# DeltaNet into a GELU MLP on one core: where the row steps stand between the weight groups, and the order of the head

## The chip, the cores and the metric

The kernel runs on one core of one Trainium2 chip. The metric is the device time of that core in microseconds (us), from its first to its last instruction. The kernel before takes 669.52 us, the median of three runs (669.08 to 671.37). The core has five engines that work side by side, each through its own list of instructions in order: PE (TensorE, matmuls), DVE (VectorE), ACT (ScalarE), POOL (GpSimd) and SP (SyncE, which issues most DMAs here). They wait for each other by semaphores only.

## The reference

Attention state by the delta rule, for 4 batches, 8 heads, 768 steps, head size 48; then a two-layer MLP with an exact GELU over 3072 tokens (384 to 2048 to 384). All is f32, but the two weight matrices come as float64.

```python
k_n = k / (np.linalg.norm(k, axis=-1, keepdims=True) + 1e-06)
for t in range(S):
    y[:, :, t] = einsum('bhd,bhde->bhe', q[:, :, t], state)
    v_old = einsum('bhde,bhd->bhe', state, k_n[:, :, t])
    state = state + beta[:, :, t] * einsum('bhd,bhe->bhde', k_n[:, :, t], v[:, :, t] - v_old)
x = y.transpose(0, 2, 1, 3).reshape(B * S, H * D)
h = x @ w_in
out = (0.5 * h * (1.0 + erf(h / sqrt(2)))) @ w_out
```

## The kernel before

**Chunks.** The 768 steps are cut into 12 chunks of 64 (`C`). Two batches share the 128 partitions, so a chunk is two units (`NA`), `tiles[c, a]`. Inside a chunk the recurrence becomes matrices: the gram matrix of the keys (`grams`, psG), the queries against the keys (`queries`, P), and a unit triangular system for each head that is inverted. Chunks go by pairs, called groups (`g`). For a group, `eliminate_steps(g)` inverts the 32x32 diagonal blocks of all heads on DVE: `scales` and `flip` bring the blocks into one tile Nu, 30 pairs of `row_product` (L492) and `row_sum` (L497) do the substitution one row after the other, each needing what the one before wrote; `diagonal` and `back` (L506, L510) turn the result into XM and Zf. `join` makes of two 32-blocks one of 64 by two matmuls (psJ), with a product on DVE between (L542, later L583).

**A chunk's pass.** `against_state` multiplies the keys and queries with the state (psK) and W = (psK - V) times factors on DVE (L658, L659). `solve` gives U (psU), `use` gives the output psY and the state's change (`update`), `next_state` adds it on DVE (L708), `read` copies the output to x, and `turn` transposes x into xT (psX, L740). V has to be scaled by the norm of its key first: of chunk 0 in `ng`, of chunk 1 by POOL (`scale_v`, L362), of chunks 2 and 3 by ACT, one head at a time (`scale_head`, L357), of the later ones by POOL. `prep(c)` makes the squares of a chunk's keys on ACT (L303), their sums on DVE (L308) and the root on POOL (L334); `finish(c)` turns them into factors on DVE.

**The MLP.** `fc1` is one of 16 tiles of the first layer (psH, L763), its GELU on ACT writes G (L765). `fc2` is the second layer (psO, L776) for chunks 0 and 1; later chunks use a scheme with seven half products (L801), with sums of w_out on DVE (`sums_of_w`, L787).

**The weights.** The float64 words come in as pairs of 32-bit words and are decoded on chip, in 16 groups of 128 x 768: groups 0 to 7 are w_in, 8 to 15 w_out. `fetch(n)` loads a group's raw words, into four places in w_out_sb for w_in, into three slots for w_out; a place is loaded again when its group has been scaled. A group takes five DVE steps and one on ACT: `begin` (L220, exponent bits), `exponents` on ACT (L225), `upper` (L229), `lower` (L234), `sign` (L242, needs ACT's exponent) and `scaled` (L246). `decode_steps(first, last)` orders them so that the steps of group n and n + 1 alternate.

**What sets the order.** The head, up to the first decoded groups, is written out by hand for all engines (`by_hand`), so program order there is engine order. After it, a plan of steps with times is sorted: `on(a, b, steps)` spreads steps over a stretch on the author's own scale of time, `once(t, ...)` puts them at one time, `at` does the same on a scale of chunks. Up to `late`, DVE and ACT run in the plan's order; after it DVE alone. On the other engines a scheduler orders what the plan emits, except where `together` ties matmuls to each other and where `keep_in_program_order` holds an ACT instruction in its place. `late` frees the memory and banks of the first stage, and clears two tiles Kb on ACT (L1007) that lie there; the first layer of chunk 1 has 12 tiles ahead of it (`EARLY`) and 4 behind it.

Of the kernel before, what the change touches and what calls it, by code (L numbers as in the profile page):

```python
# [16 lines left out]
def kernel(  # L17
# [158 lines left out]
    mask_h = mask.unsqueeze(1).to_broadcast([128, H, C])  # L176
    Zf = [cpool.tile([128, NU, C], F32, name=f"Zf{i}") for i in range(2)]
    G = cpool.tile([128, NF, NA * 128], F32)
    for p in range(2):
        nc.gpsimd.memset(Zf[0][p * C + HB:(p + 1) * C, :, 0:HB], 0.0)  # L180
    St = cpool.tile([128, NA, 2, NP, D], F32)
    nc.vector.memset(St, 0.0)
    nc.scalar.activation(lim[:, 1:2], lim[:, 0:1], ACT.Gelu)
# [101 lines left out]
    def new_group(g):  # L285
        gms[g] = wk.tile([128, 2 * NA, H], F32, tag="gm", name="gm")
# [9 lines left out]
    def squares(u, n, engine=None):  # L296
        kd = u.Kn[:, :, 0:D]
        if engine is nc.gpsimd:
            ksq = su.tile([128, H, D], F32, tag="w_e", name="ksq")
        else:  # L300
            ksq = wk.tile([128, H, D], F32, tag="ksq", name="ksq")
        if engine is None:
            i = nc.scalar.activation(ksq, kd, ACT.Square)  # L303
            if u.c == 4:
                tc.keep_in_program_order(i)
        else:
            engine.tensor_tensor(ksq, kd, kd, op=ALU.mult)
        nc.vector.tensor_reduce(n, ksq, axis=AX.X, op=ALU.add)  # L308
# [52 lines left out]
    def scale_v(u, engine=nc.gpsimd):  # L361
        engine.tensor_tensor(u.V, u.V, ns[u.c][:, u.a].unsqueeze(2).to_broadcast([128, H, D]),  # L362
                                op=ALU.mult)

    def transposed(u, part=(0, 1)):
        for x in part:
            if x == 0:
                dst = u.Kt = wk.tile([128, 2, NP, C], F32, tag="Kt", name="Kt", bufs=6)
            elif u.c == 1:
                dst = u.Qt = su.tile([128, 2, NP, C], F32, tag="Qt1", name="Qt1")  # L370
            else:
                dst = u.Qt = wk.tile([128, 2, NP, C], F32, tag="Qt", name="Qt")
# [178 lines left out]

    def copy_out(name, n):
        for dst, src in copies[name][:n]:
            tc.keep_in_program_order(nc.scalar.copy(dst, src))
        del copies[name][:n]

    def join_run(g, ts0, ts1):
# [354 lines left out]
    for n in range(2):  # L912
        fetch(n)
    load_k(2, "Kp")
    new_group(0)
    n0 = wk.tile([128, 2 * NA, H], F32, tag="n0", name="n0", bufs=1)
    for c in range(2):
# [10 lines left out]
    scales_, flip_, *rows, back0, back1 = [s_[1:] for s_ in eliminate_steps(0)]  # L928
    factors(gms[0], beta_m[:, 0:2].rearrange("q c a h -> q (c a) h"), n0)
    scales_[0]()  # L930
    flip_[0]()
    ng = wk.tile([128, NA, H], F32, tag="n", name="ng", bufs=4)
    for u in first:
        grams([u])
    signs(2, NC)
    for u in first:
        transposed(u, (1,))
        queries([u])
        for h in range(4 * u.t, 4 * u.t + 4):
            sum_of_squares(tiles[2, h // H], h % H)  # L940
    for a in range(NA):
        fetch_in(tiles[2, a].Qp[:, :, 0:D], q, tiles[2, a])
    for a in range(NA):
# [2 lines left out]
        fetch(n)  # L946
    for n in range(n_in, n_in + len(slots)):
        fetch(n)
    load_v(1)
    third = [tiles[2, a] for a in range(NA)]  # L950
    for u in third:
        transposed(u, (0,))
    grams(third)
    for u in third:
        transposed(u, (1,))
    fourth = [tiles[3, a] for a in range(NA)]
    for u in fourth:
        transposed(u, (0,))
    grams(fourth)
# [10 lines left out]
    left(0, range(NA))  # L970
    for a in range(NA):
        join(0, (a,), 1)
    for step in copies.pop("diag"):
        nc.scalar.copy(*step)
    for u in first[NA:]:
        scale_v(u)
    for n in range(2):
        begin(n)
    for n in range(2):
        exponents(n)  # L980
    for n in range(2):
        mantissas(n)
    solve(first[:NA])
    signed(0)
    use(first[:NA])
    for u in first[:NA]:
        read(u)
    signed(1)
    for u in first[:NA]:
        turn(u)  # L990
    begin(2)
    exponents(2)
    mantissas(2)
    signed(2)
    by_hand.close()
    tc.no_sync_barrier()

# [21 lines left out]
    def fc1s(c, f, n, first, last):  # L1019
# [1 line left out]

    zero, one, b = first[:NA], first[NA:], range(NA, 2 * NA)
    rows1, join1 = eliminate_steps(1), join_steps(1)
    plan = [fc1s(0, 0, 4, 57.0, 63.0), fc1s(0, 4, 2, 65.0, 67.8), fc1s(0, 6, 2, 69.0, 71.8),
            fc1s(0, 8, 4, 73.6, 79.0), fc1s(0, 12, 2, 80.0, 82.8), fc1s(0, 14, 2, 85.4, 88.0)]
    plan += [once(63.2, (together, *[(update, u) for u in zero], (join, 0, b, 0)),
                  *[(next_state, u) for u in zero]),
             once(64.2, (left, 0, b)), once(68.3, (together, (join, 0, b, 1))),
             once(72.2, (together, (against_state, one))), once(75.2, (subtract, one)),
             once(79.2, (together, (solve, one))), once(83.2, (together, (use, one))),  # L1030
             once(84.6, *[(read, u) for u in one]), once(86.0, *[(next_state, u) for u in one]),
             once(88.1, *[(turn, u) for u in one])]
    plan += [on(57.8, 72.0, [(1.0, sum_of_squares, tiles[3, a], h)
                             for a in range(NA) for h in range(H)]),
             once(73.0, (load, 3), (prep, 2), (prep, 3))]
    decode = decode_steps(3, NW)
    ends = [3 + 5 * i for i in range(NW - 2)]
    plan += [on(56.8, 60.6, decode[:ends[1]]), on(60.6, 65.0, decode[ends[1]:ends[2]]),
             on(66.5, 70.8, decode[ends[2]:ends[3]]), on(70.8, 75.0, decode[ends[3]:ends[4]]),
             on(76.8, 81.0, decode[ends[4]:ends[5]]), once(81.1, (finish_both,), *[s_[1:] for s_ in rows1[:2]]),  # L1040
             on(84.2, 125.8, alternate(decode[ends[5]:], rows1[2:-3])), once(128.6, (late,))]
    for i in range(NF // 2):
        t = 89.7 + 5.2 * i
        plan += [on(t, t + 2.5, [(1.0, fc2, u, 2 * i, 2 * i + 2) for u in zero])]
        if i < EARLY // 2:
            plan += [fc1s(1, 2 * i, 2, t + 2.6, t + 5.1)]
    plan += [fc1s(1, EARLY, NF - EARLY, 128.7, 132.0),
             on(131.5, 164.0, ffn_steps(1)[4:])]
    plan += [at(c + 1, c + 2, ffn_steps(c)) for c in range(2, NC)]
    plan += [on(91.0, 124.0, [(1.0, scale_head, tiles[2, a], h) for a in range(NA) for h in range(H)]),  # L1050
             on(133.0, 150.0, [(1.0, scale_head, tiles[3, a], h) for a in range(NA) for h in range(H)])]
    s2 = state_steps(2)
    plan += [once(126.7, *[s_[1:] for s_ in rows1[-3:-1]]),
             once(131.6, (together, (against_state, third))), once(131.7, (subtract, third)),
             once(133.0, (together, join1[0])), once(133.1, rows1[-1][1:]),
             once(136.0, (together, join1[1]), (copy_out, "join", 4)),
# [30 lines left out]
    for w in range(3, NC):  # L1087
        two_ahead = w + 2 < NC
        if w % 2:
            if w == 3:  # L1090
                plan += [at(w + 0.09, w + 0.092, [(1.0, transposed, u, (1,)) for u in fourth]
                            + [(1.0, together, *gram(5))])]
            plan += [at(w + 0.25, w + 0.95, state_steps(w, (), query(w)))]
            if two_ahead:
                rows = eliminate_steps(w // 2 + 1)
                plan += [at(w - 0.16, w - 0.15, [(1.0, prep, w + 2)]),
                         at(w, w + 0.01, [(1.0, finish, w + 2)]),
                         at(w + 0.13, w + 0.18, rows[:2]), at(w + 0.18, w + 0.36, rows[2:26]),
                         at(w + 0.4, w + 1.06, rows[26:-3]), at(w + 1.07, w + 1.2, rows[-3:])]
# [48 lines left out]
```

## Time and profile before

| | before |
|---|---|
| time, median of 3 | 669.52 us |
| profiled execution, span | 666.2 us |
| PE busy | 633.7 us (95%) |
| DVE busy | 441.3 us (66%) |
| ACT busy | 223.7 us (34%) |
| POOL busy | 82.3 us (12%) |
| decode, sign (L242), mean of one | 0.95 us |
| row product (L492), mean of one | 0.34 us |

A line of the page's groups or of the timeline names the line of the kernel, the engine, the operation, out<-in by tile, shapes and count, and times; a bracket behind it says how long the engine had been idle and what ended that. L numbers are lines of the kernel before; in the kernel after, the lines from 180 to 554 stand two lower, and then within six.

### The profile page before, as it was taken

How to read it: one execution, taken by the hardware profiler on the slowest of the kernel's cores; microseconds unless marked ns; L12 is line 12 of the kernel's file. 1: busy time of each engine (PE TensorE's matmuls, PEld its weight loads, DVE VectorE, ACT ScalarE, POOL GpSimd, SP SyncE). 2: the span in 40 equal slices, each digit the busy share in tenths (PEclk: the TensorE clock that was granted, in tenths of full speed). 3: DMA queues.
4: the chain of work that ended last, by engine and by line, in shares of the span. 5: the costliest groups of instructions: out<-in, count | busy, mean ns of one | idle time of the engine just before them, and what ended most of it. 6: DMA issues, size and time to landing. Idle time of an engine off the chain costs nothing.

```text
span 666.2 us, 20430 instructions
## 1 busy us (share of the span) xinstructions
PE 633.7 (95%) x8902; PEld 555.5 (83%) x8902; DVE 441.3 (66%) x920; ACT 223.7 (34%) x600; POOL 82.3 (12%) x81
## 2 busy tenths in 40 slices
PE   6678998899999999999999999999999999999997
PEld 5566875666589989989989989989989989989997
DVE  6989999956759865578755678755678754324022
ACT  3476653334352126232136132136032133131220
POOL 5043210002401011211011211011301010000000
PEclk9986999989999999999999999999999999999999
DMA  9696554122533233521233521212301210100101
GB/s 133 156 273 173 110 104 142 47 43 46 99 46 61 49 44 51 83 43 26 53 46 49 82 42 25 51 23 37 60 12 20 55 18 3 25 2 2 25 0 25
DMA packets 158426, 39.68 MB, mean 60 GB/s; under 512 B 150016, under 2 KB 153216, under 8 KB 158336
## 3 DMA queue, kind: packets, MB, share of 16 engines
q1 hardware_dynamic: 152464, 33.40, 26.6%
q10 hardware_dynamic: 5872, 4.97, 3.4%
q8 instruction: 70, 1.15, 0.7%
q14 instruction: 20, 0.16, 0.1%
HBM read 33.62 MB, written 4.72 MB: 58 GB/s over the span
## 4 chain that ended last, share of the span: by engine, by line
PE 78%; DVE 9%; DMA 4%; SPq 3%; ACT 2%; issue 1%; POOL 1%; ACTq 0%; POOLq 0%
PE psH L763 33%; PE psX L801 12%; PE psY L801 12%; PE psZ L801 4%; PE psK L645 3%; PE psG L397 3%; PE psO L776 3%; PE psJ L571 2%; SPq L96 2%; PE psY L694 2%; PE psU L675 2%; DMA w_out_sb<-in_moe_w_in_dram 2%; DMA Kp<-in_k_dram 1%; SPq L212 1%; DVE Nu L497 1%
## 5 line engine op out<-in xcount | busy, mean ns | idle before, releaser
L763 PE MATMUL psH<-xT,w_in_sb 128*128 128x256 f32 x1152 | 260.9, 384 | 2.9 <-ACT G L765 2.3
L763 PEld LDWEIGHTS psH<-xT,w_in_sb 128*128 128x128 f32 x1152 | 217.4, 191 | 36.5 <-ACT G L765 4.1
L765 ACT ACTIVATE G<-psH 128x256 f32<-128x256 f32 x192 | 73.1, 382 | 177.3 <-PE psH L763 162.5
L497 DVE TENSOR_TENSOR Nu<-Nu,tmp 128x30 f32<-128x30 f32 (+9 forms) x180 | 62.0, 344 | 5.0
L492 DVE TENSOR_TENSOR tmp<-Nu 128x30 f32<-128x30 f32 (+9 forms) x180 | 60.6, 336 | 5.0
L801 PE MATMUL psX<-w_out_sb,G 128*128 128x192 f32 x320 | 55.8, 328 | 0.0
L801 PE MATMUL psY<-w_out_sb,G 128*128 128x192 f32 x304 | 54.1, 329 | 1.1
L740 ACT COPY xT<-psX 128x384 f32<-128x384 f32 x24 | 11.5, 479 | 126.1 <-PE psX L739 124.7
L801 PEld LDWEIGHTS psX<-w_out_sb,G 128*128 128x128 f32 x320 | 52.4, 190 | 0.6
L801 PEld LDWEIGHTS psY<-w_out_sb,G 128*128 128x128 f32 x304 | 49.1, 190 | 3.2 <-DVE u L847 3.2
L776 PE MATMUL psO<-w_out_sb,G 128*128 128x384 f32 x128 | 46.5, 511 | 5.0 <-DVE w_out_sb L246 4.3
L334 POOL TENSOR_TENSOR n<-n,half 128x16 f32<-128x16 f32 x10 | 30.9, 3086 | 127.2 <-DVE n L308 105.0
L810 DVE TENSOR_TENSOR S<-G 128x512 f32<-128x512 f32 x20 | 13.8, 691 | 46.5 <-ACT G L765 46.1
L776 PEld LDWEIGHTS psO<-w_out_sb,G 128*128 128x128 f32 x128 | 23.9, 196 | 21.9 <-DVE w_out_sb L246 6.7
L658 DVE TENSOR_TENSOR W<-psK,V 128x384 f32<-128x384 f32 x22 | 12.2, 553 | 41.8 <-ACT y L657 41.2
L460 POOL MEMSET Zf<- 32x512 f32 x20 | 10.4, 518 | 194.7 <-DVE Zf L510 128.7
L815 DVE TENSOR_TENSOR G<-G 128x512 f32<-128x512 f32 x20 | 13.7, 691 | 24.9 <-PE psX L801 24.9
L801 PE MATMUL psY<-T,G 128*128 128x192 f32 x160 | 28.2, 329 | 0.0
L801 PE MATMUL psZ<-T,S 128*128 128x192 f32 x160 | 28.1, 329 | 0.0
L801 PE MATMUL psX<-T,G 128*128 128x192 f32 x160 | 28.1, 329 | 0.0
L362 POOL TENSOR_TENSOR V<-V,n 128x384 f32<-128x384 f32 x18 | 16.1, 905 | 84.7 <-DMA V<-in_v_dram 64.0
L801 PEld LDWEIGHTS psZ<-T,S 128*128 128x128 f32 x160 | 26.1, 190 | 0.3
(146 smaller groups left out, 856.2 us busy)
## 6 DMA issues: line engine op xcount, KB each, us to landing
Kp<-in_k_dram SPq DMA_DIRECT2D x76, 96.0 KB, 3.2
w_out_sb<-in_moe_w_in_dram SPq DMA_DIRECT2D x24, 256.0 KB, 4.3
V<-in_v_dram SPq DMA_DIRECT2D x48, 96.0 KB, 3.3
out_dram<-o_sb ACTq DMA_DIRECT2D x46, 96.0 KB, 2.2
w_raw<-in_moe_w_out_dram SPq DMA_DIRECT2D x10, 384.0 KB, 3.9
Zf<-in_moe_w_out_dram SPq DMA_DIRECT2D x6, 384.0 KB, 4.5
Qp<-in_q_dram SPq DMA_DIRECT2D x64, 32.0 KB, 2.2
Qp<-in_q_dram SPq DMA_DIRECT2D x16, 96.0 KB, 4.3
```

The lines of the kernel that those rows point to most:

```text
L334: nc.gpsimd.tensor_tensor(flat, flat, half, op=ALU.pow)
L362: engine.tensor_tensor(u.V, u.V, ns[u.c][:, u.a].unsqueeze(2).to_broadcast([128, H, D]), op=ALU.mult)
L397: nc.tensor.matmul(psG[HALF[p], r, i * NP + j, :], lhsT=u.Kt[rows, p, j, :], rhs=(u.Qt if x else u.Kt)[rows, p, j, :], start=True, stop=True)
L492: nc.vector.tensor_tensor(tmp, nu[:, j + 1:, j:j + 1].to_broadcast([128, n, j]), nu[:, j:j + 1, 0:j].to_broadcast([128, n, j]), op=ALU.mult)
L497: nc.vector.tensor_tensor(nu[:, j + 1:, 0:j], nu[:, j + 1:, 0:j], tmps.pop(j), op=ALU.add)
L645: nc.tensor.matmul(u.psK[to, x, r, j, :], lhsT=(u.Qt if x else u.Kt)[rows, p, j, :], rhs=St[rows, u.a, p ^ r, j, :], start=True, stop=True)
L763: nc.tensor.matmul(psH, lhsT=w_in_sb[:, f // 2, m, f % 2 * 128:(f % 2 + 1) * 128], rhs=xTs[c][:, m, :], start=(m == 0), stop=(m == NM - 1))
L765: nc.scalar.activation(G[:, f, :], psH, ACT.Gelu)
L776: nc.tensor.matmul(u.psO, lhsT=G[:, f, u.a * 128:(u.a + 1) * 128], rhs=w_out_sb[:, f, :], start=(f == 0), stop=(f == NF - 1))
L801: nc.tensor.matmul(ps_, lhsT=lhs[:, f, :], rhs=rhs[:, f, :], start=first and f == 0, stop=f == FH - 1, skip_group_check=not first)
L810: nc.vector.tensor_tensor(W2["S"][:, fs], a21, a22, op=ALU.add)
L815: nc.vector.tensor_tensor(a12, a12, a11, op=ALU.subtract)
```

## The change

It touches the head and the first three chunks.

- Row steps of group 1: before, they alternate with the last seven and a half weight groups, up to the last decode step. After, the plan decodes up to group 9 without them, and puts the first 40 row steps between groups 10 to 15; the last 20 follow behind the last decode step. `finish_both` and the first two steps move behind group 9.
- Decoding of groups 0 to 2: the steps of groups 0 and 1 go in pairs (begin, begin, upper, upper, ...), and group 2 is part of the alternating order from its start, so that no step needs the one just ahead of it.
- The head's transposes of the queries run one tile ahead of the products that use them; of chunk 2, one transpose goes ahead of the grams.
- V of chunk 1 is loaded earlier, behind K of chunk 2, and scaled by ACT in the head, head by head; POOL's two instructions go.
- Times of the plan's other steps up to chunk 3 are set anew: six tiles of fc1 ahead of the first join, the first pair of fc2 ahead of chunk 1's turn, prep of chunk 5 later, with its squares kept in program order on ACT. The lower copies of diag for chunk 3 and the clearing of a part of Zf go later.

```diff
-    for p in range(2):
-        nc.gpsimd.memset(Zf[0][p * C + HB:(p + 1) * C, :, 0:HB], 0.0)
...
             i = nc.scalar.activation(ksq, kd, ACT.Square)
-            if u.c == 4:
+            if u.c < 6:
                 tc.keep_in_program_order(i)
...
     load_k(2, "Kp")
+    load_v(1)
...
     scales_[0]()
+    for p in range(2):
+        nc.gpsimd.memset(Zf[0][p * C + HB:(p + 1) * C, :, 0:HB], 0.0)
     flip_[0]()
...
-    for u in first:
-        transposed(u, (1,))
+    transposed(first[0], (1,))
+    for u, ahead in zip(first, first[1:] + [None]):
+        if ahead is not None:
+            transposed(ahead, (1,))
         queries([u])
         for h in range(4 * u.t, 4 * u.t + 4):
             sum_of_squares(tiles[2, h // H], h % H)
+        for h in range(4 * u.t, 4 * u.t + 4):
+            scale_head(tiles[1, h // H], h % H)
...
-    for step in copies.pop("diag"):
-        nc.scalar.copy(*step)
-    for u in first[NA:]:
-        scale_v(u)
-    for n in range(2):
-        begin(n)
-    for n in range(2):
-        exponents(n)
-    for n in range(2):
-        mantissas(n)
+    for step in (begin, exponents, upper, lower):
+        for n in range(2):
+            step(n)
     solve(first[:NA])
-    signed(0)
+    sign(0)
+    sign(1)
...
-    signed(1)
+    scaled(0)
+    scaled(1)
...
-    begin(2)
-    exponents(2)
-    mantissas(2)
-    signed(2)
+    decode = decode_steps(2, NW)
+    for _, fn, *args in decode[:3]:
+        fn(*args)
...
-    plan = [fc1s(0, 0, 4, 57.0, 63.0), fc1s(0, 4, 2, 65.0, 67.8), fc1s(0, 6, 2, 69.0, 71.8),
-            fc1s(0, 8, 4, 73.6, 79.0), fc1s(0, 12, 2, 80.0, 82.8), fc1s(0, 14, 2, 85.4, 88.0)]
+    plan = [fc1s(0, 0, 6, 57.0, 63.2), fc1s(0, 6, 2, 65.2, 67.8), fc1s(0, 8, 2, 69.2, 71.8),
+            fc1s(0, 10, 4, 74.9, 79.1), fc1s(0, 14, 2, 80.5, 83.1)]
...
-    plan += [on(56.8, 60.6, decode[:ends[1]]), on(60.6, 65.0, decode[ends[1]:ends[2]]),
-             on(66.5, 70.8, decode[ends[2]:ends[3]]), on(70.8, 75.0, decode[ends[3]:ends[4]]),
-             on(76.8, 81.0, decode[ends[4]:ends[5]]), once(81.1, (finish_both,), *[s_[1:] for s_ in rows1[:2]]),
-             on(84.2, 125.8, alternate(decode[ends[5]:], rows1[2:-3])), once(128.6, (late,))]
+    plan += [on(54.3, 57.9, group(2)), on(57.9, 61.4, group(3)), on(61.4, 65.0, group(4)),
+             on(67.5, 71.0, group(5)), on(71.0, 74.6, group(6)), on(76.8, 80.4, group(7)),
+             on(80.4, 84.0, group(8)), on(84.0, 87.5, group(9)),
+             once(87.8, (finish_both,), *[s_[1:] for s_ in rows1[:2]]),
+             on(91.9, 126.0, alternate(group(10, NW - 1), rows1[2:42])),
+             on(126.1, 128.4, rows1[42:-3]), once(128.6, (late,))]
     for i in range(NF // 2):
-        t = 89.7 + 5.2 * i
+        t = (84.2, 88.3)[i] if i < 2 else 92.1 + 5.68 * (i - 1)
...
-                plan += [at(w - 0.16, w - 0.15, [(1.0, prep, w + 2)]),
+                plan += [at(w - (0.05 if w == 3 else 0.16), w - (0.04 if w == 3 else 0.15), [(1.0, prep, w + 2)]),
```

More of the change, by code (lines that the diff above doesn't have):

```diff
@@ L553, in copy_out @@
         for dst, src in copies[name][:n]:
-            tc.keep_in_program_order(nc.scalar.copy(dst, src))
+            i = nc.scalar.copy(dst, src)
+            if name != "diag":
+                tc.keep_in_program_order(i)
         del copies[name][:n]
@@ L948 @@
         fetch(n)
-    load_v(1)
     third = [tiles[2, a] for a in range(NA)]
+    fourth = [tiles[3, a] for a in range(NA)]
     for u in third:
         transposed(u, (0,))
+    transposed(third[0], (1,))
     grams(third)
-    for u in third:
-        transposed(u, (1,))
-    fourth = [tiles[3, a] for a in range(NA)]
+    transposed(third[1], (1,))
     for u in fourth:
@@ L1023, with group @@
     rows1, join1 = eliminate_steps(1), join_steps(1)
-    plan = [fc1s(0, 0, 4, 57.0, 63.0), fc1s(0, 4, 2, 65.0, 67.8), fc1s(0, 6, 2, 69.0, 71.8),
-            fc1s(0, 8, 4, 73.6, 79.0), fc1s(0, 12, 2, 80.0, 82.8), fc1s(0, 14, 2, 85.4, 88.0)]
-    plan += [once(63.2, (together, *[(update, u) for u in zero], (join, 0, b, 0)),
+    def group(n, last=None):
+        return decode[3 + 5 * (n - 2):3 + 5 * ((last or n) - 1)]
+    plan = [fc1s(0, 0, 6, 57.0, 63.2), fc1s(0, 6, 2, 65.2, 67.8), fc1s(0, 8, 2, 69.2, 71.8),
+            fc1s(0, 10, 4, 74.9, 79.1), fc1s(0, 14, 2, 80.5, 83.1)]
+    plan += [once(65.05, (together, *[(update, u) for u in zero], (join, 0, b, 0)),
                   *[(next_state, u) for u in zero]),
-             once(64.2, (left, 0, b)), once(68.3, (together, (join, 0, b, 1))),
-             once(72.2, (together, (against_state, one))), once(75.2, (subtract, one)),
+             once(66.2, (left, 0, b), (copy_out, "diag", 2)), once(68.0, (together, (join, 0, b, 1))),
+             once(71.9, (together, (against_state, one))), once(74.7, (subtract, one)),
              once(79.2, (together, (solve, one))), once(83.2, (together, (use, one))),
-             once(84.6, *[(read, u) for u in one]), once(86.0, *[(next_state, u) for u in one]),
-             once(88.1, *[(turn, u) for u in one])]
+             once(85.2, *[(read, u) for u in one]), once(87.6, *[(next_state, u) for u in one]),
+             once(87.7, *[(turn, u) for u in one])]
     plan += [on(57.8, 72.0, [(1.0, sum_of_squares, tiles[3, a], h)
@@ L1035 @@
              once(73.0, (load, 3), (prep, 2), (prep, 3))]
-    decode = decode_steps(3, NW)
-    ends = [3 + 5 * i for i in range(NW - 2)]
-    plan += [on(56.8, 60.6, decode[:ends[1]]), on(60.6, 65.0, decode[ends[1]:ends[2]]),
-             on(66.5, 70.8, decode[ends[2]:ends[3]]), on(70.8, 75.0, decode[ends[3]:ends[4]]),
-             on(76.8, 81.0, decode[ends[4]:ends[5]]), once(81.1, (finish_both,), *[s_[1:] for s_ in rows1[:2]]),
-             on(84.2, 125.8, alternate(decode[ends[5]:], rows1[2:-3])), once(128.6, (late,))]
+    plan += [on(54.3, 57.9, group(2)), on(57.9, 61.4, group(3)), on(61.4, 65.0, group(4)),
[4 more added lines that the diff above has]
+             on(126.1, 128.4, rows1[42:-3]), once(128.6, (late,))]
     for i in range(NF // 2):
-        t = 89.7 + 5.2 * i
+        t = (84.2, 88.3)[i] if i < 2 else 92.1 + 5.68 * (i - 1)
         plan += [on(t, t + 2.5, [(1.0, fc2, u, 2 * i, 2 * i + 2) for u in zero])]
+        t = max(t + 2.6, 88.8)
         if i < EARLY // 2:
-            plan += [fc1s(1, 2 * i, 2, t + 2.6, t + 5.1)]
+            plan += [fc1s(1, 2 * i, 2, t, t + 2.5)]
     plan += [fc1s(1, EARLY, NF - EARLY, 128.7, 132.0),
-             on(131.5, 164.0, ffn_steps(1)[4:])]
+             on(131.5, 164.0, ffn_steps(1)[NF - EARLY:])]
     plan += [at(c + 1, c + 2, ffn_steps(c)) for c in range(2, NC)]
@@ L1052 @@
     s2 = state_steps(2)
-    plan += [once(126.7, *[s_[1:] for s_ in rows1[-3:-1]]),
+    plan += [once(128.5, *[s_[1:] for s_ in rows1[-3:-1]]),
              once(131.6, (together, (against_state, third))), once(131.7, (subtract, third)),
```

## The prediction

> **What bounds the kernel now.** I read the busy shares in 40 slices first, then the stretches of the opening 150 us, then VectorE's (DVE's) timeline in them, and last who waited for whom.
>
> ```profile
> PE   6678998899999999999999999999999999999997
> ...
> DVE  6989999956759865578755678755678754324022
> ...
> PEclk9986999989999999999999999999999999999999
> ```
>
> From slice 12 on (200 us) PE, TensorE, is 9 in every slice but the last, so the rest of the program has a fixed length: what counts is when it begins. Before, slices 2 to 8 are DVE's.
>
> ```profile
> 85.82:90.34 4.52, 4.52 (x140) 3.93 (x139) 4.16 (x9) 1.22 (x4) 1.91 (x1) 1.00 0.63 111
> 90.34:136.37 46.03, 40.34 (x157) 28.13 (x156) 44.08 (x100) 17.67 (x45) 0.00 (x0) 0.97 0.33 93
> 136.37:140.50 4.13, 4.13 (x14) 2.50 (x13) 4.04 (x5) 0.48 (x1) 0.00 (x0) 0.97 0.01 1
> 140.50:148.30 7.80, 6.67 (x142) 5.41 (x144) 0.03 (x1) 3.42 (x8) 0.00 (x0) 1.00 0.47 79
> ```
>
> (Columns: PE, PE's weight loads, DVE, ACT = ScalarE, POOL = GpSimd, each busy us and count; clock; DMA.) DVE is 96% busy until the last weight group is decoded, and empty right behind it. The timeline of DVE and PE there:
>
> ```profile
> 134.20 0.95 DVE L242 SCALAR_TENSOR_TENSOR w_e<-w_raw,w_e 128x768 uint32<-128x768 uint32 x1
> 135.07 0.21 DVE L497 TENSOR_TENSOR Nu<-Nu,tmp 128x58 f32<-128x58 f32 x1
> 135.32 0.19 DVE L492 TENSOR_TENSOR tmp<-Nu 128x30 f32<-128x30 f32 x1
> 135.42 0.95 DVE L246 SCALAR_TENSOR_TENSOR w_out_sb<-w_out_sb,w_e 128x768 f32<-128x768 f32 x1
> 136.57 2.07 DVE L506 STREAM_TRANSPOSE XM<-Nu 128x1024 f32<-128x1024 f32 x1
> 138.54 1.90 DVE L510 STREAM_TRANSPOSE Zf<-Nu 128x1024 f32<-128x1024 f32 x1
> 148.27 0.56 DVE L658 TENSOR_TENSOR W<-psK,V 128x384 f32<-128x384 f32 x1 [7.83 <-ACT y L657]
> ...
> 132.91 7.12 PE L776 MATMUL psO<-w_out_sb,G 128*128 128x384 f32 x16 [2.34 <-DVE w_out_sb L246]
> 143.74 2.86 PE L763 MATMUL psH<-xT,w_in_sb 128*128 128x256 f32 x12 [1.13 <-ACT G L765]
> ```
>
> The chain to read: last decode (ends 136.3), second layer of chunk 0 (psO, ends 140.0), its copies and sends, PE free at 143.74. The row steps (L492, L497) between the decode steps are needed by nobody until psJ at 148.54. DVE then idles 7.83 us: that is the room for them.
>
> **What the Trainium skill says.** "VectorE: DVE Perf Modes", section "The DRAIN you can't avoid": a next op waits until the pipe is empty, but "a next op that is not held starts earlier". The trace shows both:
>
> ```profile
> 28.11 0.41 DVE L497 TENSOR_TENSOR Nu<-Nu,tmp 128x238 f32<-128x238 f32 x1
> 28.55 0.41 DVE L492 TENSOR_TENSOR tmp<-Nu 128x240 f32<-128x240 f32 x1
> ...
> 71.49 0.95 DVE L234 SCALAR_TENSOR_TENSOR w_in_sb<-w_out_sb,w_in_sb 128x768 f32<-128x768 uint32 x1
> 72.36 0.55 DVE L220 TENSOR_SCALAR w_e<-w_out_sb 128x768 uint32<-128x768 uint32 x1
> ```
>
> Row steps need what stands just ahead: 0.41 long, the next after 0.44. The decode ops here do not: 0.95 long, the next after 0.87. So a dependent neighbour costs about 0.11 us. "GPSIMD Engine Reference", section "1. Specifications": its SBUF interfaces are shared with VectorE. The trace agrees: while POOL scales V (49.85 to 52.49) two decode ops take 1.47 and 1.58 instead of 0.95. "TensorE: Matmul & The Clock Gate", Part 1, gives half clock after an idle window; here the clock is 0.50 from 48 to 61 us and again at 134 to 136.
>
> **The change part by part.** A full decode step of one group costs 0.47+0.87+0.47+0.87+0.87 = 3.55 us from start to start (timeline, 72.36 to 75.90).
>
> 1. Groups 0 to 3. The steps of a group are begin (L220), upper (L229), lower (L234), sign (L242), scaled (L246). Before, DVE goes from the first begin at 47.33 to the end of lower of group 3 at 62.37. After: two ops of each kind at a time, 3.62 for begins, uppers, lowers and 3.48 for signs and scales, ending 54.4; no V on POOL, so no stretching. Then start 2, upper 2, lower 2, start 3: 2.4, at 56.8. Sign 2 needs ACT's exponent, which stands on ACT behind the copies of xT, and those behind psU (ended 51.98) by 6.56 us; psU had a hole of 1.55 us that no semaphore explains. With less DMA then (the fetches leave some 5 us earlier, as the Q tiles come free earlier) I take 0.5 off: exponent at 58.0, so a wait of 1.2. Ends: no wait, or 1.8. Then 3.1 to lower 3 done: 61.1, gain 1.3.
> 2. Steps between there and the row steps. Seven groups at 3.55 = 24.8 (groups 4 to 10). The join (L542) and state sums (L708) keep their 2.4 us, W its 2.1, the second sums 1.0, factors and flip 4.5 (85.82 to 90.34). Waits before: 0.46 (psJ), 0.62 (W), 1.2 (sums behind ACT's x). After: the join's psJ stands behind six first-layer tiles, not four. At half clock until 61.5 and 1.3 us a tile after that, PE reaches psJ's end at 69.5, DVE is there at 68.2: wait 1.3 (ends 0 and 2.5). For W I keep 0.3; the sums come after three more groups, when x has long been copied: 0. The row steps begin at 61.1+24.8+3.7+2.4+1.0+4.5 = 97.5. Before they began at 90.34, with two groups (7.1 us) less decoded and the second sums (2.2 with their waits) still ahead: so far 2.2 us are won.
> 3. The six last groups with row steps. 27 decode steps are left: 5 x 3.55 + 1.74 = 19.4. Of 60 row ops 38 stand ahead of the last decode op (in before, all but one). In group 0, where they run alone, these 38 take 18.44 to 32.94 = 14.5; 26 of them now have a decode op behind them, 26 x 0.11 = 2.9 less: 11.6. Last decode: 97.5+19.4+11.6 = 128.5, against 136.3: **7.8 us earlier**. The check on before: 37 x 0.71 + 59 row ops at 0.29 + 2.2 for sums = 46, as the stretch 90.34 to 136.37 has it.
> 4. The tail on PE. PE's work after psY of chunk 1 (88.7 by the same sum) is 32 matmuls of psO at 0.65 (149.62 to 152.40 holds four; the trace shows an f32 matmul twice), 20.8, psX 2.7, twelve first-layer tiles 15.6 = 39.1, so it could end at 127.8; it follows DVE by one pair, 2.6, ending 131.2, without the half clock that stretched 132.91 to 140.03. Copies, sends and Kb then as before (about 3.3): PE free at 134.4, **9.3 earlier**.
> 5. The row steps put behind: 22 ops alone take 7.4 (32.94 to 40.34), transposes 4: DVE free at 140.0 on this clock. psJ needs XM at 139.2, it is there at 138.0; W could start at 139.0, so 1.0 late, and the second psJ stands about 0.8 on PE. **1.0 back.**
> 6. ACT in the head: 16 heads of V of chunk 1 at 0.245 (L357, x4 in 0.99) = 4 us more on ACT; queued behind them are Qt, P and Kt copies that end in psJ and the first L542. The transposes one tile ahead take away the four waits of Qt for PE and of PE for Qt (ACT waited 5.0 for psG, PE 4.6 for Qt), so ACT's idle pays: Kt copies at 36.9 (before 36.85). This needs V landed by 26.5; its loads are issued from 21.4, behind the K tiles that landed at 25.2. V's landings in the trace took 3.1 to 8.8 us; I take 5.2, the median, so 26.6. At 8.8 ACT stands about 3 to 4 us, and so does all that follows.
> 7. Chunk 5's squares (prep 5) go later and stay in program order on ACT. Before, ACT held them ahead of the xT copy and PE stood 1.57 (168.64 to 170.20): about 1.3 saved. After, they come behind the last o_sb (181.10), 13 us later, and on DVE the transposes of K, the sums of w_out (5.3) and the new factors queue behind them: the flip of group 2 begins about 3 us later against PE, and W and S of chunks 2 and 3 (202 to 213), where DVE is 95% busy, make psU and psZ wait 0.6 and 1.3. **0.5 back** net, ends -1.3 and +2.
> 8. Zf's clearing after XM's scaling and the lower copies of diag later: nothing, since the flip waits for diag at 15.07 anyway, and ACT has 1.2 us less ahead of the exponents (counted in 1).
>
> Sum: -9.3 + 1.0 + 0.5 = -7.8: 669.5 - 7.8 = **661.7**.
>
> **The rivals.** (a) All early waits vanish: no wait in 1 and 2 (-2.5), squares of chunk 5 pure gain (-1.3 in place of +0.5): 661.7 - 2.5 - 1.8 = 657.4. For it: these waits are guesses on a clock state. Against: ACT and PE really are in order there. (b) PE becomes the bound between 57 and 130 (its work there is 69 of 73 us by the sums above), or V lands late: 3 to 5 us back, about 665.7. For it: three waits of 0.6 for G in before. (c) Slower: V lands at 8.8, costing 4; the flip of group 2 slips 3 us more and finds no idle on DVE; psJ waits 2.5: 669.5 - 7.8 + 4 + 3 + 1.2 (2.5 in place of 1.3) + 1.5 for Kt copies behind it = 671.4. Against it: DVE has 1.2 and 0.95 us idle at 226 to 230 that absorb part.
>
> **How the numbers follow.** Forecast 0.58, (a) 0.2, (b) 0.13, (c) 0.06, and 0.03 for a sum near nothing. The range 656.8 to 667 takes in (a), (b) and the ends of items 1, 2 and 7. The bound of 0.3% is 2 us: faster 0.89, same 0.05, slower 0.06.
>
> **What would show it.** Right: the last L246 on w_out_sb ends near 128.5; 22 row ops follow it back to back; PE free near 134; W's idle of 7.83 gone; no POOL V before 60. Wrong: a wait for DMA V on ACT before 35 that moves the first L542 past 46; L542 or sign 2 waiting over 2.5; PE standing at psU, psZ or psJ for over 3 us in sum between 135 and 225.

## The result and the profile after

The kernel after takes 663.39 us (median of four runs, 661.74 to 663.9), the kernel before beside it 669.38 (669.08 to 671.37): a ratio of 0.9900, with a 95% interval of 0.9874 to 0.9927. That is 6.0 us less, and inside the forecast range, 1.7 us above its likeliest value. The profiled pair differs by less, 666.2 to 662.1, as before's profiled execution was one of its shorter ones (667.93 us as timed), and after's one of its longer ones.

The busy shares of the kernel after, in 40 slices (16.55 us each):

```profile
PE   6578999899999999999999999999999999999997
...
DVE  7969899996299855678755679755678754324022
...
PEclk9855999999999999999999999999999999999999
```

PE (TensorE) still stands at 9 from slice 12 on. DVE (VectorE) is filled from slice 5 to 8, where before had a 5 in slice 8. Two things are new in the head: a clock at half in slices 2 and 3, and a 6 for DVE in slice 2, where before had an 8. So the end of the decoding got better, and the head got worse. First the end, by stretches (columns as before: PE, weight loads, DVE, ACT = ScalarE, POOL = GpSimd, then clock and DMA):

```profile
96.77:101.19 4.42, 4.42 (x26) 3.60 (x26) 4.06 (x9) 1.20 (x3) 1.91 (x1) 1.00 0.88 173
101.19:132.00 30.81, 28.69 (x110) 20.23 (x108) 30.39 (x67) 12.17 (x33) 0.00 (x0) 1.00 0.26 83
132.00:138.62 6.62, 5.44 (x21) 3.65 (x21) 6.00 (x20) 2.43 (x6) 0.00 (x0) 1.00 0.27 59
138.62:152.20 13.58, 13.58 (x316) 10.12 (x320) 11.94 (x20) 4.85 (x15) 2.07 (x4) 1.00 0.42 60
```

The stretch with row steps (101.19 to 132.00) is 30.8 us long, where it was 46.0; it holds fewer groups and fewer row steps than before. Behind it, DVE works on while PE finishes the second layer; before, DVE had 0.03 us of work in the 7.8 us that follow the transposes. The timeline of DVE and PE there:

```profile
131.05 0.95 DVE L244 SCALAR_TENSOR_TENSOR w_out_sb<-w_out_sb,w_e 128x768 f32<-128x768 f32 x1
131.92 0.38 DVE L490 TENSOR_TENSOR tmp<-Nu 128x220 f32<-128x220 f32 x1
...
139.15 0.19 DVE L495 TENSOR_TENSOR Nu<-Nu,tmp 128x30 f32<-128x30 f32 x1
139.31 0.09 DVE L499 MEMSET Nu<- 128x32 f32 x1
139.44 2.12 DVE L504 STREAM_TRANSPOSE XM<-Nu 128x1024 f32<-128x1024 f32 x1
141.43 1.99 DVE L508 STREAM_TRANSPOSE Zf<-Nu 128x1024 f32<-128x1024 f32 x1
143.24 0.56 DVE L658 TENSOR_TENSOR W<-psK,V 128x384 f32<-128x384 f32 x1
...
138.62 2.86 PE L763 MATMUL psH<-xT,w_in_sb 128*128 128x256 f32 x12 [1.12 <-ACT G L765]
```

22 row steps stand back to back behind the last `scaled` (L244): the 20 that the plan puts there, and the last two of the 40 ahead of them. W comes right behind Zf's transpose: its idle of 7.83 us is gone. PE's last first-layer tiles of chunk 1 begin at 138.62, where before had them at 143.74. So 5.1 us are won here, not the 9.3 that the forecast had. Of the 4.2 us that are missing, 2.7 are in the head. Its timeline in the kernel after, ACT's waits first, then the first join on DVE:

```profile
26.04 0.24 ACT L317 ACTIVATE ksq<-Kp 128x48 f32<-128x48 f32 x1 [2.42 <-DMA Kp<-in_k_dram]
28.69 1.01 ACT L355 ACTIVATE V<-V,n 128x48 f32<-128x48 f32 x4 [1.64 <-DMA V<-in_v_dram]
37.40 1.06 ACT L375 COPY Kt<-psT 128x512 f32<-128x512 f32 x2
48.22 1.75 DVE L540 TENSOR_TENSOR XM<-psJ,gm 32x256 f32<-32x256 f32 x4 [4.87 <-PE psJ L529]
```

ACT stands 4.1 us in two waits for loads. Everything behind them in ACT's order comes late, and the join, which before began at 45.55, begins at 48.22, though DVE's row steps for group 0 ended 1.05 us earlier than before. DVE stands for psJ for 4.87 us.

### The profile page after: what moved, and what is told of

Its sections match the earlier page's. It is cut to its first block, busy times and chain, and to the rows that moved or that the text cites. A ratio compares the mean times of both kernels' runs of the same rounds, so it can differ in the third digit from the quotient of the medians.

```text
span 662.1 us, 20444 instructions
## 1 busy us (share of the span) xinstructions
PE 633.9 (96%) x8902; PEld 557.3 (84%) x8902; DVE 441.3 (67%) x920; ACT 226.5 (34%) x616; POOL 77.9 (12%) x79
## 4 chain that ended last, share of the span: by engine, by line
PE 74%; DVE 14%; ACT 5%; SPq 3%; issue 2%; DMA 2%; POOL 1%; ACTq 1%; DVEq 0%; POOLq 0%
PE psH L763 31%; PE psY L801 12%; PE psX L801 11%; PE psZ L801 4%; PE psG L395 3%; PE psK L645 3%; PE psO L776 3%; PE psJ L571 2%; SPq L96 2%; DVE tmp L490 2%; DVE Nu L495 2%; PE psY L694 2%; PE psU L675 1%; DVE w_e L240 1%; PE psY L703 1%
## 5 line engine op out<-in xcount | busy, mean ns | idle before, releaser
L763 PE MATMUL psH<-xT,w_in_sb 128*128 128x256 f32 x1152 | 261.7, 385 | 2.1 <-ACT G L765 1.1
L763 PEld LDWEIGHTS psH<-xT,w_in_sb 128*128 128x128 f32 x1152 | 218.2, 192 | 36.0 <-ACT G L765 2.5
L801 PE MATMUL psY<-w_out_sb,G 128*128 128x192 f32 x304 | 54.2, 329 | 2.5 <-DVE u L844 1.4
L801 PE MATMUL psX<-w_out_sb,G 128*128 128x192 f32 x320 | 55.8, 328 | 0.0
L801 PEld LDWEIGHTS psY<-w_out_sb,G 128*128 128x128 f32 x304 | 49.1, 190 | 4.9 <-DVE u L847 3.2
L801 PEld LDWEIGHTS psX<-w_out_sb,G 128*128 128x128 f32 x320 | 52.4, 190 | 0.6
L332 POOL TENSOR_TENSOR n<-n,half 128x16 f32<-128x16 f32 x10 | 29.3, 2925 | 151.0 <-DVE n L306 117.4
L776 PE MATMUL psO<-w_out_sb,G 128*128 128x384 f32 x128 | 44.8, 493 | 2.2 <-DVE w_out_sb L244 2.1
L810 DVE TENSOR_TENSOR S<-G 128x512 f32<-128x512 f32 x20 | 13.8, 691 | 46.2 <-ACT G L765 45.8
L801 PE MATMUL psY<-T,G 128*128 128x192 f32 x160 | 28.2, 329 | 0.0
L801 PE MATMUL psZ<-T,S 128*128 128x192 f32 x160 | 28.1, 329 | 0.0
L801 PE MATMUL psX<-T,G 128*128 128x192 f32 x160 | 28.0, 329 | 0.0
L801 PEld LDWEIGHTS psZ<-T,S 128*128 128x128 f32 x160 | 26.1, 190 | 0.3
L801 PEld LDWEIGHTS psX<-T,G 128*128 128x128 f32 x160 | 26.1, 190 | 0.2
```

The source lines that it names most:

```text
L332: nc.gpsimd.tensor_tensor(flat, flat, half, op=ALU.pow)
L763: nc.tensor.matmul(psH, lhsT=w_in_sb[:, f // 2, m, f % 2 * 128:(f % 2 + 1) * 128], rhs=xTs[c][:, m, :], start=(m == 0), stop=(m == NM - 1))
L776: nc.tensor.matmul(u.psO, lhsT=G[:, f, u.a * 128:(u.a + 1) * 128], rhs=w_out_sb[:, f, :], start=(f == 0), stop=(f == NF - 1))
L801: nc.tensor.matmul(ps_, lhsT=lhs[:, f, :], rhs=rhs[:, f, :], start=first and f == 0, stop=f == FH - 1, skip_group_check=not first)
L810: nc.vector.tensor_tensor(W2["S"][:, fs], a21, a22, op=ALU.add)
```

## The experiments

All ratios are to the kernel before run beside them on the same chip, with 95% intervals. "From the first begin to the last decode" is DVE's way from the first L218 (L220 in before's numbering) to the end of the last L244 (L246); "PE free" is the begin of the last L763 matmuls of chunk 1; "tail" is from there to the begin of the last of chunk 2's three psY products (L801), near 220 us. From that begin to the end it took 438.4 to 439.6 us in all twelve traces.

| kernel | ratio | first join | begin to last decode | PE free | tail |
|---|---|---|---|---|---|
| before | 1 | 45.55 | 89.0 | 143.74 | 83.5 |
| after | 0.9900 (0.9874 to 0.9927) | 48.22 | 82.0 | 138.62 | 84.6 |
| after again | 0.9900 (0.9884 to 0.9916) | 47.39 | 81.7 | 137.46 | 84.5 |
| row steps alone | 0.9884 (0.9869 to 0.9900) | 46.34 | 82.9 | 137.66 | 83.7 |
| V on GpSimd | 0.9846 (0.9830 to 0.9861) | 44.20 | 82.6 | 135.17 | 84.6 |
| K, V loads first | 0.9839 (0.9824 to 0.9853) | 43.80 | 81.7 | 133.88 | 84.6 |
| squares back | 0.9875 (0.9855 to 0.9895) | 45.35 | 81.6 | 135.38 | 83.2 |
| loads first, rows all between | 0.9964 (0.9947 to 0.9980) | 43.78 | 88.7 | 140.93 | 84.5 |
| loads first, squares in the middle | 0.9824 (0.9811 to 0.9838) | 43.39 | 81.2 | 133.02 | 82.3 |
| the same, fewer rows ahead | 0.9823 (0.9808 to 0.9838) | 43.67 | 79.1 | 131.13 | 84.9 |
| loads first, pairs undone | 0.9848 (0.9832 to 0.9863) | 44.46 | 81.8 | 134.68 | 84.5 |
| loads first, transposes back | 0.9904 (0.9887 to 0.9921) | 48.43 | 81.5 | 138.30 | 84.5 |

**The row steps alone, in the kernel before.**

```diff
-             on(84.2, 125.8, alternate(decode[ends[5]:], rows1[2:-3])), once(128.6, (late,))]
+             on(84.2, 91.8, decode[ends[5]:38]),
+             on(91.9, 126.0, alternate(decode[38:], rows1[2:42])),
+             on(126.1, 128.4, rows1[42:-3]), once(128.6, (late,))]
...
-    plan += [once(126.7, *[s_[1:] for s_ in rows1[-3:-1]]),
+    plan += [once(128.5, *[s_[1:] for s_ in rows1[-3:-1]]),
```

> The kernel before with the row-step move alone: groups 8 and 9 decoded without row steps, 40 row operations among the last six groups, 21 behind the last decode step. Theory (the row steps behind the last decode carry the gain): the last L246 on w_out_sb ends 7.4 us earlier, near 128.9; the first layer of chunk 1 leaves PE free near 136.4 instead of 143.74; the 7.8 us of DVE idle ahead of W shrink to under 1; total 662.3 (661.5 to 664.0), so about what all parts of the change give together. Rival (the gain comes from the pairing of decode steps, from V off GpSimd and from the head; row steps only move the wait to psJ): total 666 to 669.

662.57 us: this one edit gives as much as the whole change. Its last decode ended at 131.04, not at 128.9: the head itself came 0.8 us later in this execution than in that of before (46.34), and from the first begin on 6.1 us were saved, not 7.4. The rival is out. It follows that all the rest of the change came, in sum, to nearly nothing, and the next runs ask which part of it lost what another won.

**V of chunk 1 back on GpSimd.**

```diff
     load_k(2, "Kp")
-    load_v(1)
...
-        for h in range(4 * u.t, 4 * u.t + 4):
-            scale_head(tiles[1, h // H], h % H)
...
+    load_v(1)
     third = [tiles[2, a] for a in range(NA)]
...
+    for u in first[NA:]:
+        scale_v(u)
     for step in (begin, exponents, upper, lower):
```

> The changed kernel with V of chunk 1 back on GpSimd and its loads back behind the weight fetches. Theory (V's heads on ScalarE and their early loads cost the head 2.7 us): no wait for DMA V on ScalarE, the first L540 at 44.5 to 46.0 instead of 48.22, clock 1.0 again in most of 30 to 41 us; but GpSimd stretches one or two decode steps (about 1.2 us back), so the last decode ends 1 to 2 us earlier and the total is 661.9 (661.0 to 663.0). Rival (the half clock and the head come from the order of the transposes, not from V): the first L540 stays at 47.5 to 48.5 and the stretched decode steps come on top: 664 to 665.

660.08 us, better than expected: the first join came right behind Zf's transpose, at 44.20, with no wait. The price is on the timeline of DVE and POOL in this run:

```profile
45.98 2.52 DVE L218 TENSOR_SCALAR w_e<-w_out_sb 128x768 uint32<-128x768 uint32 x2
48.42 1.68 DVE L227 TENSOR_SCALAR w_in_sb<-w_out_sb 128x768 uint32<-128x768 uint32 x2
...
46.93 2.26 POOL L360 TENSOR_TENSOR V<-V,n 128x384 f32<-128x384 f32 x2
```

Two begins take 2.52 us and two uppers 1.68, where the pairs take 1.03 and 1.02 in after. The Trainium skill, "GPSIMD Engine Reference", section "1. Specifications", says that GpSimd's SBUF interfaces are shared with VectorE, with contention for VectorE instructions in a 2-port performance mode or with two SBUF inputs. The trace agrees that the two get in each other's way; begins and uppers have one SBUF input, and whether they run in that mode no run here shows. The rival, that the order of the transposes spoilt the head, is out.

**The loads of K and V ahead of the weight fetches.**

```diff
     load_v(0)
-    for n in range(2):
-        fetch(n)
     load_k(2, "Kp")
     load_v(1)
+    for n in range(2):
+        fetch(n)
```

> The changed kernel with the six weight fetches issued behind the loads of K of chunk 2 and V of chunk 1 instead of ahead of them; nothing else. Theory (ScalarE in the head stands 2.42 us for Kp and 1.64 us for V because these loads are issued at 20.2 and 22.8 us, behind 3.9 us of fetch issues on SyncE's queue): both waits go to under 0.5, Kt copies of chunk 2 start near 34 instead of 37.4, the first L540 at 44.5 to 45.8 instead of 48.22, the clock is not at half all through 30 to 45; total 660.6 (659.5 to 662.0). Rival 1 (the head is bound by TensorE at half clock or by ScalarE's 4 us of V): waits go but the first L540 comes at 47 or later and the total stays within 1 us of the changed kernel. Rival 2 (the weight fetches come late now): the first begin (L218) waits for a DMA and the total is longer.

659.38 us. No engine but SyncE changed its order. The timeline of this run, ACT and DVE as above:

```profile
24.17 0.25 ACT L317 ACTIVATE ksq<-Kp 128x48 f32<-128x48 f32 x1
25.09 1.00 ACT L355 ACTIVATE V<-V,n 128x48 f32<-128x48 f32 x4
33.78 1.07 ACT L375 COPY Kt<-psT 128x512 f32<-128x512 f32 x2
43.80 1.75 DVE L540 TENSOR_TENSOR XM<-psJ,gm 32x256 f32<-32x256 f32 x4
```

Both waits are gone, the Kt copies begin 3.6 us earlier, and the join waits for nothing: now DVE's own row steps bind. This is the theory's case, and 1.2 us more than it asked for. So ACT did have the 4 us for V. What it lacked was the data: in after, SyncE spent 3.9 us on the six fetch issues ahead.

**The head's transposes back, on that version.**

```diff
-    transposed(first[0], (1,))
-    for u, ahead in zip(first, first[1:] + [None]):
-        if ahead is not None:
-            transposed(ahead, (1,))
+    for u in first:
+        transposed(u, (1,))
         queries([u])
...
-    transposed(third[0], (1,))
     grams(third)
-    transposed(third[1], (1,))
+    for u in third:
+        transposed(u, (1,))
```

> V and K loads ahead of the weight fetches, with the head's transposes of Q no longer one tile ahead (each tile's transposes right ahead of its own products, the third tile's behind its grams). Theory (they take ScalarE's four waits of 1.25 us for psG away, and that idle is what pays for V's 16 heads, 4 us): the waits of 1.25 us are back, the copies that end in psJ come 4 to 5 us later, the first L540 at 47 to 48.5 instead of 43.8, total 659.4 + 3.5 = 662.9 (661.5 to 664.5). Rival (ScalarE has room in the head without them once the loads are early): the first L540 within 1 us of 43.8, total 659 to 660.5.

663.46 us, as the theory had it. ACT in this run:

```profile
23.48 0.58 ACT L432 COPY P<-psG 128x512 f32<-128x512 f32 x1 [1.25 <-PE psG L395]
27.59 0.58 ACT L432 COPY P<-psG 128x512 f32<-128x512 f32 x1 [1.25 <-PE psG L395]
```

The four waits of 1.25 us are there again (two are shown), and the join is at 48.43. So the transposes one tile ahead are worth 4 us once V is on ACT, and in the kernel after they were spent on waiting for its loads.

**The pairs undone, on that version.** Groups 0 and 1 use `mantissas` and `signed` again:

```diff
-    for step in (begin, exponents, upper, lower):
+    for step in (begin, exponents, mantissas):
...
-    sign(0)
-    sign(1)
+    signed(0)
     use(first[:NA])
...
-    scaled(0)
-    scaled(1)
+    signed(1)
```

> V and K loads ahead of the weight fetches, with groups 0 and 1 decoded in the order of before (upper and lower of a group together, sign and scaled of a group together) instead of operation by operation over both groups. Theory (a neighbour that depends on the one ahead costs 0.11 us more; four such neighbours appear): VectorE is 0.4 us later at the begin of group 2, total 659.4 + 0.4 = 659.8 (659.2 to 660.6). Rival (the gain of 1.6 us that this stretch showed came from the pairing itself and not from V being off GpSimd): total 661.0 (660.5 to 662).

From the join to the begin of group 2 DVE takes 10.13 us instead of 9.65: the 0.4 us expected, and too little for the total to show (0.9848 against 0.9839). The rival is out. In after this stretch takes 8.88 us, in before 10.51, so 1.63 less. This run puts 0.48 of that down to the pairs; before's two decode operations beside POOL's V, 1.47 and 1.58 instead of 0.96 and 0.95, account for the other 1.14. (The 9.65 of the loads-first run has 0.77 us in it by which POOL's masks stretch the begins.) The forecast tied the price of a dependent neighbour to the operation that its quoted section calls held; the runs show the price, 0.12 us for each of the four here, but not that reason.

**All row steps between the groups, on that version.**

```diff
-             on(91.9, 126.0, alternate(group(10, NW - 1), rows1[2:42])),
-             on(126.1, 128.4, rows1[42:-3]), once(128.6, (late,))]
+             on(91.9, 126.0, alternate(group(10, NW - 1), rows1[2:-3])), once(128.6, (late,))]
```

> V and K loads ahead of the weight fetches, and in addition all 61 row operations spread among the last six groups, none left behind the last decode step: every part of the change but that. Theory (what stands behind the last decode step carries the gain): the last L244 ends 7.0 us later than with the 21 behind it (127.3 there), near 134.3, DVE stands idle about 7 us ahead of W, and the total is 659.4 + 6.5 = 665.9 (664.5 to 667.0). Rival (with the head mended TensorE alone sets the end of that stretch, it was busy 5.0 of 5 us up to 118): total 659.4 to 662.

666.17 us. DVE in this run:

```profile
133.26 0.95 DVE L244 SCALAR_TENSOR_TENSOR w_out_sb<-w_out_sb,w_e 128x768 f32<-128x768 f32 x1
...
145.45 0.56 DVE L658 TENSOR_TENSOR W<-psK,V 128x384 f32<-128x384 f32 x1 [6.93 <-ACT y L657]
```

Only the last two row steps are still behind the last decode. It ends 7.0 us later, and W's idle is back with 6.93 us, both as expected. With the run of the row steps alone this settles the main point from two sides: adding the edit to before takes 1.16% off, taking it out of a better version puts 1.25% on.

**The squares of chunk 5 back.**

```diff
-            if u.c < 6:
+            if u.c == 4:
...
-                plan += [at(w - (0.05 if w == 3 else 0.16), w - (0.04 if w == 3 else 0.15), [(1.0, prep, w + 2)]),
+                plan += [at(w - 0.16, w - 0.15, [(1.0, prep, w + 2)]),
```

> The changed kernel with the squares of chunk 5 back at their former time and free in ScalarE's order. Theory (later squares save TensorE a stand of 1.3 us at psX but cost 1.4 us at psY of chunk 3, L801, that waits for u, L844): the wait of 1.5 us at psX near 163 is back and the wait of 1.43 us at psY near 220 is gone; total within 0.7 us of the changed kernel (663.4). Rival (the wait at psY has another cause, and later squares are pure gain): total 1 to 1.6 us longer, 664.4 to 665.0, with psY's wait still there.

Both waits moved as the theory said (the psY meant is chunk 2's). PE in after:

```profile
163.30 0.52 PE L739 MATMUL psX<-ident,x 128*128 128x128 f32 x3 [0.36 <-DVE x L718]
219.94 2.87 PE L801 MATMUL psY<-w_out_sb,G 128*128 128x192 f32 x16 [1.43 <-DVE u L844]
```

and with the squares back:

```profile
161.62 0.55 PE L739 MATMUL psX<-ident,x 128*128 128x128 f32 x3 [1.30 <-ACT xT L740]
...
215.41 2.77 PE L801 MATMUL psY<-w_out_sb,G 128*128 128x192 f32 x16
```

The tail is 1.4 us shorter than in after. Counted from PE free, the later squares of after bring the first L801 only 0.4 us forward (64.0 us against 64.4), and between it and this psY they cost 1.7. So this part of the change lost more than it won. The total alone would not show it: 662.47 us, with an interval that overlaps that of after. The head of the profiled execution was a good one (join at 45.35, 659.47 us; the other four took 662.44 to 662.52), so only the tail is compared.

That head shows one thing more, as its program is the same as after's. V's first head began 1.49 us earlier on ACT, the join 2.87 us earlier. The other 1.38 us lie on PE. In after:

```profile
44.14 1.11 PE L374 MATMUL psT<-ident,Qp 128*128 128x128 f32 x4 [1.19 <-ACT Qt L375]
45.18 1.99 PE L395 MATMUL psG<-Kt 48*64 48x64 f32 x64
47.10 1.92 PE L529 MATMUL psJ<-XM,G 32*32 32x32 f32 x64
```

and here:

```profile
42.65 0.66 PE L374 MATMUL psT<-ident,Qp 128*128 128x128 f32 x4 [1.18 <-ACT Qt L375]
43.24 1.44 PE L395 MATMUL psG<-Kt 48*64 48x64 f32 x64
44.61 1.20 PE L529 MATMUL psJ<-XM,G 32*32 32x32 f32 x64
```

**The squares in the middle, on the version with the loads first.** They go behind the copies of diag and ahead of the second o_sb copy:

```diff
-                plan += [at(w - (0.05 if w == 3 else 0.16), w - (0.04 if w == 3 else 0.15), [(1.0, prep, w + 2)]),
+                plan += [at(w - (0.2 if w == 3 else 0.16), w - (0.19 if w == 3 else 0.15), [(1.0, prep, w + 2)]),
```

> V and K loads ahead of the weight fetches, and the squares of chunk 5 on ScalarE behind the two xT copies and the copies of G and diag but ahead of the second o_sb copy of chunk 1. Theory (squares ahead of xT cost 1.3 us at psX, squares behind o_sb make DVE's flip of group 2 wait and cost 1.4 us at psY, L801): neither wait is there, total 659.4 - 1.2 = 658.2 (657.3 to 659.0). Rival (the wait at psY of chunk 3 has another cause): total 659.4 within 0.5, psY still waiting over 1 us for u.

657.04 us. PE in this run has neither wait:

```profile
157.68 0.52 PE L739 MATMUL psX<-ident,x 128*128 128x128 f32 x3 [0.36 <-DVE x L718]
...
212.09 2.77 PE L801 MATMUL psY<-w_out_sb,G 128*128 128x192 f32 x16
```

The tail is 82.3 us, the shortest of all, 2.3 less than in the loads-first run. The ratios, 0.9824 and 0.9839, differ by 1.0 us, and their intervals overlap, so the size of this gain is known from the trace only. It is a version that beats both kernels, by 1.8% and 0.8%.

**Fewer row steps ahead of the last decode, on that.** `rows1[2:42]` and `rows1[42:-3]` become `rows1[2:36]` and `rows1[36:-3]`.

> As the run before this one in the list, with 34 row operations among the last six groups and 27 behind them instead of 40 and 21. Theory (TensorE waited 1.03 and 1.12 us for the last two pairs of decoded columns, and XM's transpose had about 2 us to spare ahead of psJ): the last decode ends 2.2 us earlier, TensorE's waits for w_out_sb nearly vanish, psJ and W come right behind XM and Zf and give about half of it back: 1.0 us shorter than that run (0.2 to 2.0). Rival (the XM transpose is already the bound): no gain or up to 1 us longer, with a new wait of TensorE for XM at psJ.

656.49 us and the same ratio: no gain. The last decode ends 2.2 us earlier relative to the first begin, and PE's waits for w_out_sb are gone, but PE has new ones:

```profile
136.86 1.15 PE L571 MATMUL psJ<-XM,G 32*64 32x64 f32 x32 [0.86 <-DVE XM L504]
141.45 0.32 PE L571 MATMUL psJ<-Zf,XM 32*64 32x64 f32 x2 [0.67 <-DVE XM L583]
142.44 0.24 PE L571 MATMUL psJ<-XM,G 32*64 32x64 f32 x1 [0.67 <-DVE XM L583]
```

These waits sum to 2.2 us. What PE no longer waits for decoded columns, it waits for XM. The theory asked for half of the gain to stay. The rival had it: no gain, and a new wait for XM at psJ. With 22 row steps behind the last decode the order is as good as with 28.

**The kernel after once more.**

> The changed kernel once more, beside the other three on one chip. Theory (its head depends on whether Kp of chunk 2 and V of chunk 1, issued late, land before ScalarE needs them; one run of the kernel with the squares put back had the first L540 at 45.35 and 659.5 us, its other runs 662.5): runs spread between 659.5 and 664, and those at the long end have TensorE at half clock from about 27 to 65 us and the first L540 at 48. Rival (the 48.22 of the first profile was the rule): all runs within 1 us of 663.4, the first L540 at 48 to 48.5 again.

662.04 us (660.55 to 663.24), so the runs do spread, but the bad head is the rule: the join is at 47.39, behind waits of 1.97 us for Kp and 1.08 us for V. Between the two traces these waits are the whole difference: V's first head begins at 27.86 here and at 28.69 in the first, 0.83 us apart, and so are the joins. For the executions without a trace it is not shown. Where the first trace has a clock of 0.50 from 30 to 65 us, the records of this one stand at 1.00 throughout, as in this line (columns PE, clock, DMA) and this one of its timeline:

```profile
45.00:50.00 5.00, 4.80 (x177) 1.00 0.20 72
...
44.36 1.99 PE L395 MATMUL psG<-Kt 48*64 48x64 f32 x64
```

The durations say otherwise. psG's 64 matmuls take 1.99 us, to the digit what they take in the first trace at a recorded 0.50; from 150 us on they take 1.16. So PE ran at half speed here too, and the clock cannot be what sets the two heads 0.8 us apart.

## Why the prediction was right, and where its sizes were off

The sum was -9.3 until PE is free, then +1.0 and +0.5. Measured in the profiled pair it is -5.1, then +0.1 and +1.1, and -4.1 at the end; the medians give -6.0. So the total came out nearer to the forecast than its steps did. By its steps:

| step | predicted | measured in after |
|---|---|---|
| 1: first begin to lower of group 3 | 13.8 | 13.4 |
| 1: sign 2 waits for ACT's exponent | 1.2 | 0.72 |
| 2: from there to the row steps | 36.4 | 37.8 |
| 3: row steps and decode steps | 31.0 | 30.8 |
| 4: last decode to PE free | 5.9 | 6.6 |
| 5: the row steps behind | 1.0 back | 0.1 (PE free to psU 13.58, before 13.51) |
| 6: first begin | 47.33, as before | 50.00 |
| 7: squares of chunk 5 | 0.5 back | 1.1 back |

- **The mechanism held.** Row steps that nobody needs yet stood ahead of the decoding that sets the end; behind it they fill DVE's idle. Two runs show it with 1.16% and 1.25%, and the length of the stretch came out within 0.2 us. Of the signs named for it, W's idle is gone, 22 row steps follow back to back and POOL has no V before 60 us; but the last decode ended at 132.0 and not near 128.5, and PE was free at 138.6 and not near 134.
- **Step 6 was mis-sized, by 2.7 us.** It took Kt's copies at 36.9 and nothing late behind them. They ended at 38.46. The step counted one wait, V's, by its usual time from issue to landing, and put the issue at 21.4. But SyncE got to it at 22.83: two issues of Q at 10 us took it 2.54 us, where before had 1.31, and all behind them came 1.4 to 1.6 us later than in before. V's first head began at 28.69. Kp, for which ACT waits first, was left out; its wait became 2.42 us. The other 1.1 us were lost on PE, which ran at half speed up to psJ and beyond. From the end of these copies to the join it took 9.76 us, before 8.70, and 8.38 in the run with the squares back, with after's order but a faster PE. Its eight transposes of Q took 1.97 us, where before had a pair of tiles in 1.09 at 38 us; its psG took 1.99 (before 1.71), its psJ 1.92 (before 1.20). The Trainium skill, "TensorE: Matmul & The Clock Gate", Part 1, gives half clock after an idle window. The trace agrees: four transposes took 0.66 us at 24.75, then PE stood 4.81 us, and four took 1.11 us at 38.03. But such a stand is not needed: with the loads first, where PE stood no longer than 2.02 us from 14 us on, four took 1.11 or 1.12 all the same, up to 34.42. What kept PE slow there stays open. The forecast had named this wait as what would prove it wrong ("a wait for DMA V on ACT before 35 that moves the first L542 past 46"), and priced it under rivals (b) and (c).
- **Step 2 was 1.4 us short.** The joins' psJ cost 2.07 us instead of 1.3 and W's wait 0.80 instead of 0.3. Of the six first-layer tiles ahead of psJ more ran at half speed than assumed (36 matmuls in 10.92 us).
- **Step 4 was 0.7 us short.** The last pair of psO took 2.85 us instead of 2.6, and what lies behind it 3.7 us, as in before, where the forecast read 3.3.
- **Step 5 charged 1.0 us that nobody paid.** XM's transpose ended at 141.56 and psJ could not begin before 143.42 anyway, as PE had psK ahead of it. With the decoding 3.5 us later than forecast and PE 4.2, DVE was not the late one. In the run with fewer rows ahead, where DVE is, 2.2 us were paid.
- **Step 7 was right in sign, at half the size.** It expected stands at psU and psZ; there were none. DVE came late some 14 us behind that psZ, at psY (1.43 us, behind u).

The terms close: 2.7 (step 6), 1.4 (step 2), 0.7 (step 4), less 0.4 and 0.2 (steps 1 and 3) make the 4.2 us by which PE came free too late; less 0.9 (step 5) and 0.6 more (step 7), the misses sum to 3.9 us, against 3.7 between -7.8 and -4.1.

## What to carry to other kernels

Sort the work of a busy engine by who waits for it, and put what has no reader yet behind what sets the end, as far as its own reader stays unheld: here up to 22 row steps, while 28 only moved the wait to the next matmul. Work given to an engine that idles costs nothing only if its data are there at that point of its order, so read when the queue gets to issue the load, and what is issued ahead of it. And judge an edit by stretches between fixed events: the tail showed 1.4 us here that the total, with a head that varies by 3 us, hid.

## What the hardware showed that was not expected

- The clock records are not always to be believed: they stood at 1.00 in an execution whose psG took 1.99 us for 64 matmuls, as at a recorded 0.50, and 1.16 us later on. The trace of before has it too: four transposes took 1.11 us at 20.95 and eight took 1.09 at 38.05, with a recorded clock of 1.00 at both, so the forecast, which read half clock from 48 us on, missed that PE was at half speed in much of the head already. Durations of equal matmuls are the better witness.
- GpSimd slows one-input operations of VectorE as well: two begins took 1.03 us alone, 1.80 beside GpSimd's masks of P (loads first) and 2.52 beside masks and V (V on GpSimd), a factor of 2.4, where before's two-input operations beside V went from 0.95 to 1.58 at most.
- SyncE's issues of 96 KB took 0.7 to 1.3 us each, as means of four. Changing the order of its queue alone moved V's first head on ACT from 28.69 to 25.09.
